# One fused attention and token-mixing kernel: the order of all work from a list scheduler in the program, evacuations on ACT or DVE by load, and kv from 65-column products

## The chip, the cores and the metric

The kernel runs on one core of one Trainium2 chip. The time is device microseconds of that core; the reported figure is a median of several executions. On one core a run more than 1.5% above the fastest of the same kernel counts as slow. The kernel before took 138.2 us (median of three runs, 137.22 to 140.5); the run that was profiled has a span of 134.9 us.

## The reference

Two stages. First a linear attention with cosine weights over 8 batches of 8 heads, 576 positions and 64 channels; then a token-mixing layer whose weights are computed from its own input.

```python
def phi(x, c, s):                        # c, s: cos and sin of pi/2 * position/576
    r = np.maximum(x, 0.0)
    return np.concatenate([r * c, r * s], axis=-1)
kv  = einsum('bhsf,bhsd->bhfd', phi(k), v);   z = sum over s of phi(k)
num = einsum('bhsf,bhfd->bhsd', phi(q), kv)
den = einsum('bhsf,bhf->bhs',  phi(q), z)[..., None] + 1e-06
x   = (num / den).transpose(0, 2, 1, 3).reshape(8, 576, 512)   # then, for each batch:
W   = 1/8 * (x @ w_q) @ (x @ w_k).T
out = relu(W @ x) @ w_out                # 8 x 576 x 512, float32
```

## The kernel before

Four heads are one step H (16 steps, two for a batch). A step goes: casts of q, k and v on GpSimd (POOL in the profile); kp = relu(k) times cosine and sine, on VectorE (DVE); a transpose of q on TensorE (PE) and its evacuation on DVE; the kv products on PE; the copy of kv to SBUF on ScalarE (ACT); two num products on PE; two norms on DVE. Two steps behind, the mixing layer of earlier batches runs in the gaps, and its output leaves as 36 row tiles of 128 rows (nine for a pair of batches, "1.5" is tile 5 of pair 1). The order of all this is written by hand as one loop. PE's results land in PSUM; copying them out to SBUF is called evacuation below. The tail is what follows the kv copy of the last step, H = 15. Loads and stores share one DMA queue, the one that SP issues, but for a k load at the start and five half stores at the end, which ACT issues.

```python
inp     = ctx.enter_context(tc.tile_pool(name="inp", bufs=4))      # raw q, k, v
prep    = ctx.enter_context(tc.tile_pool(name="prep", bufs=2))     # kp and rk
outpool = ctx.enter_context(tc.tile_pool(name="outpool", bufs=4))  # finished output tiles
...
def kv_mm(H, lo, hi):
    for c in range(lo, hi):
        for w in range(2):               # cosine or sine part
            for r in range(2):           # two halves of 64 rows, side by side in PE
                nc.tensor.matmul(        # 64 x (2 heads x 65) at once: 130 columns
                    bank(K0 + r)[:, 0, w * KW:(w + 1) * KW]...,
                    kp[H][half_rows(r), c, w, :],
                    v_bufs[H % 3][half_rows(r), c, :, 0:D + 1], ...)

def kv_evac(H, eng):
    kv_sb = small.tile([P, 2, 2 * KW], BF16, name="kv_sb")
    copy(eng, kv_sb, bank(K0, 2)[:, :, 0:2 * KW])       # one copy of 520 elements
...
def wout(bp, rt0, n, m, eng, qs=(nc.sync, nc.sync)):
    o_sb = outpool.tile([P, 2, DM], FP32, name="o_sb")
    ...                                  # four matmuls a row tile
    copy(eng, o_sb[:, 0:n, :], o_ps)
    ...                                  # two stores of 64 rows, from SP
```

Half of each kv product isn't used: it also multiplies one head's keys with the other head's values.

## Time and profile before

| | PE | DVE | ACT | POOL |
|---|---|---|---|---|
| busy, us of 134.9 | 109.3 | 91.4 | 74.3 | 71.1 |
| what fills it | matmuls of all stages | q evacuation, norm, kp | copies out of PSUM | casts of q, k, v |

First the groups of instructions (line, engine, operation, shapes, count | busy us, mean ns of one | idle before and who ended it), kv products and kp product:

```profile
L238 PE MATMUL ps<-v_buf,kp 64*128 64x130 bf16 x576 | 22.8, 218 | 8.4 <-DVE qpt_buf L230 5.6 <-issue 2.7
L201 DVE TENSOR_TENSOR kp<-rk,cossin 128x2304 bf16<-128x2304 bf16 x15 | 21.0, 1403 | 1.1 <-POOL rk L188 0.9
```

Then the list of waits (who <- for whom: us in total, times, longest), reduced to the one line in which an engine waits for a store:

```profile
ACT o_sb L175 <- DMA out_dram<-o_sb: 0.6, 1, 0.6
```

By the time a tile wants a buffer, its old store has landed, but once. And the clock row of the page, granted TensorE clock in tenths for 40 slices of 3.37 us:

```profile
PEclk9999968997799999999999999999999999999998
```

### The profile page before, as it was taken

The numbers are of one execution on the slowest core, as the hardware profiler recorded it, in microseconds if no ns is written. First come the engines' busy times: TensorE is split into PE (matmuls) and PEld (weight loads), VectorE is DVE, ScalarE is ACT, GpSimd is POOL, SyncE is SP. The second block draws the span as 40 slices with busy tenths as digits, with TensorE's granted clock in tenths as the row PEclk, the third lists the DMA queues.
The fourth block names the chain that finished last, engine by engine and source line by source line (L and its number), as shares of the span: only waits on it lengthen the run. The fifth ranks groups of instructions, "written<-read, shape, count | busy, mean of one in ns | idle before, by whom it ended". The sixth has DMA issues, their size and how long they took to land.

```text
span 134.9 us, 5317 instructions
## 1 busy us (share of the span) xinstructions
PE 109.3 (81%) x2276; PEld 69.5 (52%) x2276; DVE 91.4 (68%) x147; ACT 74.3 (55%) x126; POOL 71.1 (53%) x114
## 2 busy tenths in 40 slices
PE   5839399466669989999979794999998999898840
PEld 2216275344557656766665563666765675353410
DVE  1162979746798898879986968399879854334640
ACT  6941031307656766775766474658674776754310
POOL 7637865975999999637656565479521000000000
PEclk9999968997799999999999999999999999999998
DMA  3999999999999979999999999989955442287384
GB/s 102 361 385 392 372 355 390 386 390 389 388 384 393 392 225 301 367 385 395 374 357 376 322 357 388 372 249 353 238 202 118 109 94 66 57 256 177 81 248 137
DMA packets 21143, 39.40 MB, mean 292 GB/s; under 512 B 2944, under 2 KB 4480, under 8 KB 21120
## 3 DMA queue, kind: packets, MB, share of 16 engines
q1 hardware_dynamic: 20448, 38.08, 83.1%
q10 hardware_dynamic: 672, 0.98, 2.1%
q8 instruction: 18, 0.29, 1.0%
q14 instruction: 5, 0.04, 0.1%
HBM read 29.62 MB, written 9.44 MB: 290 GB/s over the span
## 4 chain that ended last, share of the span: by engine, by line
PE 40%; DMA 28%; ACT 9%; DVE 7%; issue 6%; POOL 5%; SPq 1%; ACTq 1%; DVEq 0%
PE ps L363 17%; DMA qf<-in_q_dram 10%; DMA vf<-in_v_dram 9%; DMA wo_f<-in_moe_w_out_dram 8%; PE ps L238 7%; PE ps L298 4%; PE ps L326 4%; ACT o_sb L175 4%; PE ps L257 3%; DVE qpt_buf L230 3%; ACT mix_sb L349 3%; POOL v_buf L213 2%; PE ps L341 2%; ACT wkj L175 1%; POOL rq_buf L188 1%
## 5 line engine op out<-in xcount | busy, mean ns | idle before, releaser
L363 PE MATMUL ps<-wo_sb,mix_sb 128*128 128x512 bf16 x144 | 36.0, 380 | 2.2 <-ACT o_sb L175 0.6
L213 POOL TENSOR_SCALAR v_buf<-vf 128x640 bf16<-128x640 f32 (+2 forms) x29 | 23.0, 811 | 16.3 <-DMA vf<-in_v_dram 9.2
L238 PE MATMUL ps<-v_buf,kp 64*128 64x130 bf16 x576 | 22.8, 218 | 8.4 <-DVE qpt_buf L230 5.6
L175 ACT COPY o_sb<-ps 128x512 f32<-128x512 f32 (+1 forms) x29 | 18.3, 630 | 19.6 <-PE ps L363 15.9
L188 POOL TENSOR_SCALAR rq_buf<-qf 128x640 bf16<-128x640 f32 (+2 forms) x31 | 23.7, 779 | 9.6 <-DMA qf<-in_q_dram 8.4
L201 DVE TENSOR_TENSOR kp<-rk,cossin 128x2304 bf16<-128x2304 bf16 (+2 forms) x17 | 22.6, 1327 | 7.1 <-ACT rk L186 6.0
L272 DVE TENSOR_TENSOR x_sb<-ps,rec 128x640 bf16<-128x640 f32 x32 | 26.4, 824 | 1.1
L238 PEld LDWEIGHTS <-kp 64*128 64x128 bf16 x576 | 18.8, 94 | 11.3 <-issue 6.9
L188 POOL TENSOR_SCALAR rk<-kf 128x640 bf16<-128x640 f32 (+2 forms) x29 | 20.8, 734 | 3.6 <-DMA kf<-in_k_dram 3.2
L230 DVE TENSOR_TENSOR qpt_buf<-ps,cst 128x1152 bf16<-128x1152 bf16 x32 | 22.6, 748 | 0.0
L363 PEld LDWEIGHTS <-mix_sb 128*128 128x128 bf16 x144 | 12.6, 97 | 15.2 <-issue 1.8
L349 ACT ACTIVATE mix_sb<-ps 128x576 bf16<-128x576 f32 x30 | 19.4, 654 | 1.4 <-PE ps L341 1.4
L175 ACT CAST kv_sb<-ps 128x520 bf16<-128x520 f32 x16 | 9.5, 592 | 17.8 <-PE ps L238 17.6
L257 PEld LDWEIGHTS <-qpt_buf 64*128 64x128 bf16 x640 | 13.3, 96 | 9.2 <-issue 8.7
L270 DVE RECIPROCAL rec<-ps 128x10 f32<-128x10 f32 x32 | 7.0, 219 | 16.1 <-PE ps L263 15.8
L257 PE MATMUL ps<-kv_sb,qpt_buf 64*128 64x65 bf16 x640 | 15.8, 194 | 1.9 <-ACT kv_sb L175 1.3
L175 ACT COPY xT_buf<-ps 128x512 bf16<-128x512 bf16 x16 | 9.4, 587 | 2.8 <-PE ps L284 2.7
L102 PE MATMUL ps<-warm 128*128 128x512 bf16 x28 | 9.3, 475 | 1.5 <-DVE warm L98 1.5
L298 PE MATMUL ps<-xT_buf,wqk_sb 128*128 128x288 bf16 x64 | 9.3, 286 | 1.2 <-ACT xT_buf L175 0.7
L341 PE MATMUL ps<-wT_buf,kx 64*128 64x288 bf16 x32 | 8.8, 289 | 1.2 <-DVE kx L177 0.5
L177 DVE COPY xT_buf<-ps 128x640 bf16<-128x640 bf16 x16 | 7.7, 483 | 2.3 <-PE ps L284 2.3
L341 PE MATMUL ps<-wq,kx 64*128 64x288 bf16 x32 | 8.8, 290 | 0.0
(50 smaller groups left out, 98.2 us busy)
## 6 DMA issues: line engine op xcount, KB each, us to landing
qf<-in_q_dram SPq DMA_DIRECT2D x15, 576.0 KB, 7.1
kf<-in_k_dram SPq DMA_DIRECT2D x15, 576.0 KB, 8.0
vf<-in_v_dram SPq DMA_DIRECT2D x15, 576.0 KB, 7.7
out_dram<-o_sb SPq DMA_DIRECT2D x55, 128.0 KB, 3.9
out_dram<-o_sb SPq DMA_DIRECT2D x6, 256.0 KB, 5.3
wo_f<-in_moe_w_out_dram SPq DMA_DIRECT2D x1, 1024.0 KB, 11.3
out_dram<-o_sb ACTq DMA_DIRECT2D x5, 128.0 KB, 2.7
kf<-in_k_dram ACTq DMA_DIRECT2D x1, 320.0 KB, 4.4
```

The costliest lines, as they stand in the source:

```text
L175: nc.scalar.copy(dst, src)
L188: eng.tensor_scalar(dst, src, FMAX, 0.0, op0=ALU.min, op1=ALU.max)
L201: nc.vector.tensor_mul(kp[H][:, lo:hi], rks[H][:, lo:hi].rearrange("p c i d -> p c (i d)").unsqueeze(2) .to_broadcast([P, hi - lo, 2, 2 * D]),
L213: eng.tensor_scalar(dst, src, 1.0, 1.0, op0=ALU.mult, op1=ALU.mult)
L230: nc.vector.tensor_mul(qpt_bufs[H % 2][:, r, :, D:SLOTS * D], bank_h(K0 + r)[:, 0:1, 0:HC].to_broadcast([P, 2, HC]), cst)
L238: nc.tensor.matmul(bank(K0 + r)[:, 0, w * KW:(w + 1) * KW].rearrange("p (i e) -> p i e", i=2), kp[H][half_rows(r), c, w, :], v_bufs[H % 3] ...
L257: nc.tensor.matmul(nb[t][:, u, :], qpt_bufs[H % 2][half_rows(t), r, w, u * P:(u + 1) * P], kvs[H][half_rows(t), r, o:o + D + 1], start=(u ...
L272: nc.vector.tensor_tensor(xv[:, h, r], nv[:, :, :, 0:D], rec.to_broadcast([P, 2, SC, D]), op=ALU.mult)
L298: nc.tensor.matmul(bank(m + nh)[:, 0, 0:hs], wqk_sb[:, dmc, :, :], xT_bufs[b % 2][:, dmc, nh * hs:(nh + 1) * hs], start=(dmc == 0), stop=( ...
L341: nc.tensor.matmul(bank(m + r)[:, 0, 0:hs], kxs[b][half_rows(r), i * P:(i + 1) * P], rhs, start=True, stop=True)
L349: nc.scalar.activation(dst, src, AF.Relu, scale=scale_moe)
L363: nc.tensor.matmul(o_ps[:, r, :], mixs[bp][:, dmc, rt * P:(rt + 1) * P], wo_sb[:, dmc, :], start=(dmc == 0), stop=(dmc == NDM - 1))
```

## The change

Its intent: a list scheduler in the program, fed with a cost for every piece of work and its dependencies, orders everything, so that each engine always takes the piece that can start soonest. Each copy out of PSUM may go to ACT or DVE, whichever the plan sees free. The kv products have 65 columns, the used half only; the sine part then lies in the other 64 partitions, and two small copies move it.

```diff
+PLAN = dict(mk=1.5, pa=3.218, pc=3.9, pm=3.2, pw=1.86, pb=0.0, flex=.163, poe=4.5, ...)
+def plan_order(NB, par=None):
...
+    op(("load", nm, H), {"DMA": 1.51}, [ago(H > 4, "r" + nm, H - 4)])
+    op(("mk", H), {"DVE": par["mk"]}, [("rk", H), ago(H > 1, "kv", H - 2)], par["pmk"])
+    op(("kve", H), {"ACT": 1.05, "DVE": .8}, [("kv", H)], 3)
...
+    op(("wo", p, rt), {"PE": .86}, need, pw, "full", 1)
+    op(("oe", p, rt), {"ACT": .60, "DVE": .71}, [("wo", p, rt)], par["poe"], ...)
+    op(("st", p, rt), {"DMA": .67}, [("oe", p, rt)])
...
     def kv_mm(H):
+        for c in range(C9):
+            for i in range(2):
                 for r in range(2):
                     nc.tensor.matmul(
+                        bank(K0 + r)[:, 0, i * (D + 1):(i + 1) * (D + 1)],
+                        kp[H][half_rows(r), 2 * c + i, :, :],
+                        v_bufs[H % 3][half_rows(r), c, i, 0:D + 1], ...)
     def kv_evac(H, eng):
+        copy(eng, kv_sb, src[:, :, 0:KW])                       # 260 elements
+        copy(eng, kv_sh[0:64], src[64:128, :, 0:D + 1])         # 130
+        copy(eng, kv_sh[64:128], src[0:64, :, D + 1:KW])        # 130
...
     def wout_evac(bp, rt, m, eng):
+        o_sbs[bp, rt] = outpool.tile([P, DM], FP32, name="o_sb")   # bufs=4, as before
...
+    for n, eng, m in plan_order(NB):
+        emit(n, eng, None if m is None else M0 + m)
```

"mk" (the kp product) waits for the kv products two steps back because there are two kp buffers. The output evacuation "oe" has no such line for its four buffers.

## The prediction

> **What bounds the kernel now.** I read the page's busy rows first, then its slices, then windows of the last third, then the order of time on single engines.
>
> ```profile
> PE 109.3 (81%) x2276; PEld 69.5 (52%) x2276; DVE 91.4 (68%) x147; ACT 74.3 (55%) x126; POOL 71.1 (53%) x114
> ...
> PE   5839399466669989999979794999998999898840
> ...
> DMA  3999999999999979999999999989955442287384
> GB/s 102 361 385 392 372 355 390 386 390 389 388 384 393 392 225 301 367 385 395 374 357 376 322 357 388 372 249 353 238 202 118 109 94 66 57 256 177 81 248 137
> ```
>
> A slice is 134.9 / 40 = 3.37 us. The DMA row is full from slice 2 to about slice 30 (100 us), then idles. PE has holes up to about 43 us and is then nearly full until 129 us. So two bounds follow each other: loads, then matrix work. DVE, at 68%, looks harmless on average. By stage it is not:
>
> ```profile
> 90.00:95.00 5.00, 4.89 (x131) 3.54 (x131) 4.44 (x8) 3.87 (x6) 3.93 (x5) 1.00 0.95 314
> ...
> 100.00:105.00 5.00, 4.42 (x106) 2.68 (x98) 4.92 (x8) 2.98 (x6) 1.31 (x2) 1.00 0.47 111
> ...
> 110.00:115.00 5.00, 4.77 (x74) 2.55 (x74) 1.88 (x4) 3.19 (x7) 0.00 (x0) 1.00 0.37 86
> ```
>
> (The last column is GB/s; the engines are PE, PEld, DVE, ACT, POOL.) In 100 to 105 us DVE is busy 4.92 of 5 us. After the last attention block (110 us) it has little to do. In order of time, ACT's copies of kv date the 16 attention steps H = 0 to 15:
>
> ```profile
> 51.23 0.59 ACT L175 CAST kv_sb<-ps 128x520 bf16<-128x520 f32 x1 [1.21 <-PE ps L238]
> 57.14 0.59 ACT L175 CAST kv_sb<-ps 128x520 bf16<-128x520 f32 x1
> ...
> 85.18 0.59 ACT L175 CAST kv_sb<-ps 128x520 bf16<-128x520 f32 x1
> ...
> 110.10 0.59 ACT L175 CAST kv_sb<-ps 128x520 bf16<-128x520 f32 x1
> ```
>
> These are H = 6, 7, 11 and 15: some 6.5 us a step. From 110.1 on PE works 18.7 us more (last matmul 128.8), then 6.1 us of copy, store and end. Whatever the change does early only counts if it moves the 110.1 or shortens these 25 us.
>
> **What the skill says.** (1) "TensorE: Matmul & The Clock Gate", section "Wait — 56ns, not 53.3ns?": warm matmuls start N / 2.4 GHz + about 2.5 ns apart, so 57 ns at 130 columns and 30 ns at 65. The trace agrees if the two 64-row halves run as a pair: 35 products of 130 columns took 1.20 us up to the end of the last (17.5 pairs of 57 ns are 1.0, and one is 0.22 long), and 20 num products of 65 columns pass in 0.31 us (31 ns a pair). (2) "ScalarE: Activation LUTs", section "What ACT_TABLE_LOAD costs": an ACTIVATE with immediate scale and bias takes 186 ns + 0.833 ns an element. Here 520 elements took 592 ns and 256 took 373: slope 0.83, constant 160; I use 160. (3) "VectorE: DVE Perf Modes", section "Mode 2×_1P — pack two bf16 into one 32-bit read": two results a cycle with 16-bit, unit-step operands. The kp product (2304 elements, 1403 ns, 0.61 ns each) agrees; runs of 64 in place of 128 should not change it.
>
> **The change, part by part.**
> Kv products: 576 stay 576, with 65 columns for 130. A step goes from about 1.2 to 0.6 us: 16 x 0.55 = 8.8 us of PE removed, all before 110 us, none in the tail.
> Kv copy: one of 520 elements becomes 260 + 130 + 130: 377 + 268 + 268 = 913 ns on ACT, +0.32 us on the kv-to-num chain and 14 x 0.32 = 4.5 us of ACT busy (two steps go to DVE). The chain gets 0.6 shorter on PE, so it breaks even or better.
> Kp product, q evacuation, norm: unchanged on DVE (1403, 2 x 748, 219 + 824 ns). Start to start they are a little shorter:
>
> ```profile
> 48.49 1.41 DVE L230 TENSOR_TENSOR qpt_buf<-ps,cst 128x1152 bf16<-128x1152 bf16 x2
> 49.82 0.21 DVE L270 RECIPROCAL rec<-ps 128x10 f32<-128x10 f32 x1
> 50.06 0.82 DVE L272 TENSOR_TENSOR x_sb<-ps,rec 128x640 bf16<-128x640 f32 x1
> 50.80 1.46 DVE L201 TENSOR_TENSOR kp<-rk,cossin 128x2304 bf16<-128x2304 bf16 x1
> ```
>
> A q pair is 1.33 us, a norm 0.98, a kp 1.35 (busy 1.40, its end overlapped by the next): 1.35 + 1.33 + 2 x 1.0 = 4.7 us of DVE a step.
> Order: loads run ahead. In the built order the first output store stands behind the load of q for H = 10 (before: of k for H = 8), and the last v load still has 25 of 36 row tiles' stores behind it.
> Output tiles: still four buffers. The scheduler's list gives an output evacuation one dependency only, its matmuls. The built program adds the real one: the fifth evacuation (now on DVE) waits until the first store has **landed**, the sixth (ACT) for the second, and so on. All stores are in the same queue as the loads.
>
> That is the step I weigh most. Landing times follow from bytes. The first 12 slices sum to 4294 x 3.37 = 14.5 MB by 40.5 us, at 388 GB/s in the last six. An offset of about 1.0 us from bytes to start comes from q of H = 1 (2.36 MB, reached at 8.8 us):
>
> ```profile
> 9.84 1.15 POOL L188 TENSOR_SCALAR rq_buf<-qf 128x1152 bf16<-128x1152 f32 x1 [2.16 <-DMA qf<-in_q_dram]
> ```
>
> Through the first row tile's store: ten steps of 3 x 0.59 MB, weights 1.31, q 0.59, store 0.26 = 19.9 MB, so 40.5 + 5.4 / 0.388 + 1 = 55.3 us. DVE would want that evacuation at about 47 us (my chaining of row durations: kv of H = 4 near 33 us for 38, since ACT's four wo casts no longer stand before kv of H = 3). So I expect DVE, and then PE behind it, to idle some 8 us, throwing away the early lead; kv of H = 7 comes near 60 (before 57).
> The same repeats: row tile 1.5 (DVE) waits for store 1.1, which has 15 steps, two loads, weights and 11 stores up to its end: 31.9 MB, 40.5 + 17.4 / 0.388 + 1 = 86.4 us. After it DVE, in order, has 9 norms (9.0), 5 q pairs (6.7), 3 kp (4.0), 2 wq copies (0.7), one kv copy (0.9), one xT (0.4), the evacuation itself (0.65): 22.4 us before kv of H = 15 can start, so 108.8, and 109.4 with its products. Before it was 110.1. Of the 8.8 us of PE removed, under 1 arrives.
> Tail: 14 output row tiles are left after kv of H = 15, before 13: 18.7 + 0.95 = 19.7 us. The nine last evacuations are all on ACT (0.59 each), which also issues five half stores (0.54 each), against 0.93 a tile on PE: about 1 us of lag. 109.4 + 19.7 + 6.1 + 1 = 136.2 us of span against 134.9; in the metric 138.2 x 136.2 / 134.9 = 139.5. I take 138.5, because DVE may be packed closer, or the stores land sooner, than I chained.
>
> **Rivals.**
> A: the store waits hardly bite, because DMA interleaves better than one queue in order. Then PE or DVE sets the pace: kv of H = 6 near 44 us and 9 steps of 5.4 give 93, plus 27 is 120 of span, 123 us. For it: POOL, ACT and PE have room. Against it: the waits are in the built program and the bytes cannot come earlier.
> B: worse than mine. ACT's own waits (tiles 1.2, 1.3, 1.6 before kv copies of H = 10 and 11) hold PE, whose clock row already shows less than full after early holes; 3 to 5 us more, 142 to 144. For it: ACT is in order and carries nearly all copies. Against: DVE needs that time anyway.
> C: the DVE-only limit without gaps from 55.3 on: 8 kp (10.8), 17 norms (17.0), 9 q pairs (12.0), 4 wq copies (1.3), 5 xT (2.1), 2 output copies (1.3), one kv (0.9), 45.4 us to kv of H = 15, so 101, + 26.8 = 128 of span, 131 us. It needs store 1.1 before 80 us, beyond 388 GB/s.
>
> **Range and chances.** My sum says 139.5, C's floor 131, B 144; the tuned-looking constants of the plan suggest that someone saw a gain, which I let pull a little. Range 131.5 to 143. Faster by over 2% (below 135.4) needs the waits to be smaller than the bytes say: 0.27. Slower by over 2% (above 141): 0.23. Within: 0.50.
>
> **What would show it.** Right: the fifth output evacuation on DVE and the sixth on ACT start only near 55 us with a DMA of an output store as releaser; a hole of several us in DVE and PE at 47 to 55; kv copies of H = 7 near 61, H = 10 near 85, H = 15 near 109; DMA row full without the dip of slice 15; kv products near 0.6 us a step; 900 ns for the three kv copies. Wrong: output evacuations that never wait for a DMA; kv of H = 15 before 103 us; or a tail much under 25 us.

## The result, and the profile after

The changed kernel takes 143.79 us (median of four runs, 142.93 to 144.09). The kernel before has 137.71 in the same comparison. The ratio of fast runs is 1.0462, with a 95% interval from 1.0385 to 1.0539: slower. (Such a ratio is the mean time of one kernel's fast runs over that of the other's fast runs of the same rounds, so it is not quite the ratio of the medians.) The range of the prediction ended at 143.0; the result lies just outside.

The page of the kernel after, busy row and the rows by slice (3.54 us each):

```profile
PE 111.5 (79%) x2257; PEld 66.1 (47%) x2279; DVE 97.9 (69%) x148; ACT 80.2 (57%) x159; POOL 64.2 (45%) x76
...
PE   5857688697999581897979479998899799989920
PEclk9999968965599959559999987999999999999995
DMA  4999999999999999999999999553333703857874
```

The same list of waits, for stores, after (14.4 us in all, where before it was 0.6):

```profile
ACT o_sb L329 <- DMA out_dram<-o_sb: 8.6, 4, 3.9
DVE o_sb L331 <- DMA out_dram<-o_sb: 5.8, 1, 5.8
```

The DMA row stays full through slice 25, without the dip that the kernel before had at slice 15: loads do run ahead. PE has two holes instead: slices 14 and 16, with the digits 5 and 1 (46 to 57 us), and slice 23 with the 4 (78 to 81 us). The views by time say whose they are. First hole, all engines in order of start (start us, duration, engine, line, operation, [idle before <- releaser]):

```profile
56.23 0.69 DVE L331 COPY o_sb<-ps 128x512 f32<-128x512 f32 x1 [5.78 <-DMA out_dram<-o_sb]
56.89 0.59 ACT L329 COPY o_sb<-ps 128x512 f32<-128x512 f32 x1 [3.89 <-DMA out_dram<-o_sb]
57.37 1.84 PE L456 MATMUL ps<-xT_buf,wqk_sb 128*128 128x288 bf16 x7 [3.60 <-DVE xT_buf L331]
```

Tile 0.4 on DVE is released by a store at 56.23, tile 0.5 on ACT right after, PE last: it had waited for a piece of DVE's that stands behind the tile. Second hole:

```profile
81.21 0.59 ACT L329 COPY o_sb<-ps 128x512 f32<-128x512 f32 x1 [3.42 <-DMA out_dram<-o_sb]
82.13 0.29 PE L502 MATMUL ps<-wT_buf,kx 64*128 64x288 bf16 x1 [2.74 <-ACT kx L329]
86.32 1.15 POOL L367 TENSOR_SCALAR v_buf<-vf 128x1152 bf16<-128x1152 f32 x1 [4.58 <-PE ps L391]
86.34 2.33 DVE L355 TENSOR_TENSOR kp<-rk,cossin 128x2304 bf16<-128x2304 bf16 x1 [1.39 <-PE ps L391]
89.06 0.69 DVE L331 COPY o_sb<-ps 128x512 f32<-128x512 f32 x1
```

ACT's tile 1.2 waits for a store, PE waits for the kx copy behind it, and DVE and POOL wait for PE's kv products. DVE's kp product then takes 2.33 us, because POOL's cast started 0.02 us before it, and tile 1.5 comes at 89.06. The attention steps, dated by ACT's kv copies of H = 6, 7, 11 and 15 as before:

```profile
50.21 0.38 ACT L329 CAST kv_sb<-ps 128x260 bf16<-128x260 f32 x1
64.57 0.38 ACT L329 CAST kv_sb<-ps 128x260 bf16<-128x260 f32 x1 [0.63 <-PE ps L391]
...
92.88 0.38 ACT L329 CAST kv_sb<-ps 128x260 bf16<-128x260 f32 x1 [0.21 <-PE ps L391]
...
115.40 0.38 ACT L329 CAST kv_sb<-ps 128x260 bf16<-128x260 f32 x1 [0.42 <-PE ps L391]
```

One step, from 50.21 to 64.57, takes 14.4 us. Before, H = 15 came at 110.10; now at 115.40, and 26.3 us follow (before 24.8). The windows that the prediction showed of before (PE, PEld, DVE, ACT, POOL, clock, DMA share, GB/s), here of after:

```profile
90.00:95.00 5.00, 4.87 (x144) 3.55 (x145) 4.90 (x7) 3.54 (x9) 3.53 (x4) 1.00 0.74 161
100.00:105.00 5.00, 4.46 (x126) 3.25 (x120) 4.82 (x8) 3.70 (x9) 0.00 (x0) 1.00 0.33 69
110.00:115.00 5.00, 4.00 (x148) 2.98 (x142) 4.10 (x9) 3.35 (x6) 0.00 (x0) 1.00 0.50 107
```

From 110 to 115 us DVE is still busy with attention, which it had left behind in the kernel before. The groups, kp product and kv products:

```profile
L355 DVE TENSOR_TENSOR kp<-rk,cossin 128x2304 bf16<-128x2304 bf16 x15 | 25.9, 1726 | 4.1 <-POOL rk L342 2.0 <-PE ps L391 1.8
L391 PE MATMUL ps<-v_buf,kp 64*128 64x65 bf16 x576 | 14.2, 199 | 3.1 <-DVE qpt_buf L383 3.1
```

PE's kv products fell from 22.8 to 14.2 us, as intended. The kp product, which nobody changed in size, rose from 1403 to 1726 ns. The Trainium skill's page "SBUF — State Buffer", section "Who interferes with whom", says why it can: a DVE instruction with two SBUF inputs contends with a GpSimd instruction that reads SBUF, and the ports that they share are an exclusive lock. The trace agrees, if DVE, second to start, waited for POOL to end: from POOL's end at 86.32 + 1.15 = 87.47 to DVE's end at 86.34 + 2.33 = 88.67 are 1.20 us, and a free kp product takes 1.35. The prediction had not used that page.

### The profile page after: what moved, and what is told of

It reads as the page before. It is cut to its first block, busy times and chain, and to the rows that moved or that the text cites. A ratio compares the mean times of both kernels' runs of the same rounds, so it can differ in the third digit from the quotient of the medians.

```text
span 141.7 us, 5312 instructions
## 1 busy us (share of the span) xinstructions
PE 111.5 (79%) x2257; PEld 66.1 (47%) x2279; DVE 97.9 (69%) x148; ACT 80.2 (57%) x159; POOL 64.2 (45%) x76
## 4 chain that ended last, share of the span: by engine, by line
DMA 51%; PE 19%; issue 9%; DVE 7%; ACT 4%; POOL 3%; ACTq 2%; SPq 1%; POOLq 0%; DVEq 0%
DMA qf<-in_q_dram 13%; DMA kf<-in_k_dram 12%; PE ps L526 10%; DMA wo_f<-in_moe_w_out_dram 9%; DMA wq_f<-in_moe_w_q_dram 8%; DMA vf<-in_v_dram 6%; DMA out_dram<-o_sb 3%; ACT o_sb L329 2%; PE ps L416 2%; DVE qpt_buf L383 2%; ACTq L536 2%; POOL rk L342 2%; PE ps L456 1%; PE ps L502 1%; PE ps L486 1%
## 5 line engine op out<-in xcount | busy, mean ns | idle before, releaser
L329 ACT COPY o_sb<-ps 128x512 f32<-128x512 f32 x34 | 20.0, 588 | 23.2 <-PE ps L526 13.4
L342 POOL TENSOR_SCALAR rq_buf<-qf 128x1152 bf16<-128x1152 f32 (+2 forms) x17 | 20.6, 1214 | 18.2 <-PE ps L377 10.2
L367 POOL TENSOR_SCALAR v_buf<-vf 128x1152 bf16<-128x1152 f32 x15 | 20.6, 1375 | 14.8 <-PE ps L391 11.7
L416 PEld LDWEIGHTS <-qpt_buf 64*128 64x128 bf16 x640 | 15.1, 99 | 15.0 <-issue 13.9
L342 POOL TENSOR_SCALAR rk<-kf 128x1152 bf16<-128x1152 f32 x15 | 19.0, 1270 | 1.5 <-DMA kf<-in_k_dram 1.4
L416 PE MATMUL ps<-kv_sh,qpt_buf 64*128 64x65 bf16 x320 | 17.1, 198 | 1.1
L329 ACT COPY xT_buf<-ps 128x512 bf16<-128x512 bf16 (+1 forms) x24 | 15.1, 643 | 2.8 <-PE ps L441 2.2
L391 PE MATMUL ps<-v_buf,kp 64*128 64x65 bf16 x576 | 14.2, 199 | 3.1 <-DVE qpt_buf L383 3.1
L391 PEld LDWEIGHTS <-kp 64*128 64x128 bf16 x576 | 11.8, 100 | 7.4 <-issue 3.3
L329 ACT CAST kv_sb<-ps 128x260 bf16<-128x260 f32 x14 | 5.3, 378 | 14.3 <-PE ps L391 14.1
L329 ACT CAST wT_buf<-ps 128x576 bf16<-128x576 f32 x8 | 5.1, 639 | 8.9 <-PE ps L456 8.9
```

The lines of the kernel that those rows point to most:

```text
L329: nc.scalar.copy(dst, src)
L342: eng.tensor_scalar(dst, src, FMAX, 0.0, op0=ALU.min, op1=ALU.max)
L367: eng.tensor_scalar(dst, src, 1.0, 1.0, op0=ALU.mult, op1=ALU.mult)
L391: nc.tensor.matmul(bank(K0 + r)[:, 0, i * (D + 1):(i + 1) * (D + 1)], kp[H][half_rows(r), 2 * c + i, :, :], v_bufs[H % 3][half_rows(r), c, ...
L416: nc.tensor.matmul(nb[t][:, u, :], qpt_bufs[H % 2][rows, r, w, u * P:(u + 1) * P], mv, start=(u == 0 and w == 0), stop=False)
```

## The experiments

Sixteen different kernels (two of them again in more rounds) test what the waits for stores, the kv part, the kp product, the choice of engine and the tail each do. All gave correct results.

### e1: twelve output buffers

```diff
-    outpool = ctx.enter_context(tc.tile_pool(name="outpool", bufs=4))
+    outpool = ctx.enter_context(tc.tile_pool(name="outpool", bufs=12))
```

> The changed kernel with 12 output buffers in place of 4, nothing else. Theory (the evacuations of the output projection wait for stores that stand behind loads): the 5.8 us wait of DVE at 56 us and ACT's 8.6 us of waits for output stores vanish, the kv copies of H = 7 and H = 15 come near 52 and 97 us (64 and 115 in the changed kernel), and the time falls to 124 to 130 us, below the kernel before. Rival 1 (the loss comes from slower DVE products of kp, 1613 ns for 1403, the PE clock and the three-part kv copy): the time stays at 140 or more. Rival 2 (loads running ahead is itself the harm, since stores are late whatever the buffers): 135 to 139, with a longer tail.

133.11 us (132.72 to 133.38, four runs), 10.7 us under the changed kernel, and under every run of the kernel before in all rounds (lowest 134.69). Tile 0.4 and tile 1.5 on DVE, and the kv copy of H = 15, in e1:

```profile
52.00 0.69 DVE L331 COPY o_sb<-ps 128x512 f32<-128x512 f32 x1 [1.36 <-PE ps L526]
...
79.01 0.67 DVE L331 COPY o_sb<-ps 128x512 f32<-128x512 f32 x1
...
105.22 0.38 ACT L329 CAST kv_sb<-ps 128x260 bf16<-128x260 f32 x1 [0.37 <-PE ps L391]
```

In its list of waits no engine waits half a microsecond for a store any more, and kv of H = 15 comes 10.2 us earlier. So the waits for stores carry the whole loss. But note 79.01 to 105.22: 26.2 us, in a kernel without any such wait; the prediction packed this stretch into 22.4 + 0.6.

### e2: stores taken before loads; e4: both

The other way to get stores out earlier: when a store and a load could start alike, the plan takes the store.

```diff
-                    key = s - par["pb"] * o["prio"]
+                    key = s - par["pb"] * o["prio"] - (.01 if n[0] == "st" else 0)
```

> The changed kernel with 4 output buffers, but the scheduler takes a store before a load where both could go. Theory: the first store is issued before the load of q for H = 7 or so and lands near 46 us, so the fifth evacuation hardly waits; 127 to 133 us; the DMA row may dip where the queue waits for an evacuation. Rival 1: 140 or more. Rival 2: it gains too, but no more than to 136, since the queue then stands still for stores.

> Both: 12 output buffers and stores before loads. Theory: no evacuation waits for a store in either, so the same as with 12 buffers alone within 2 us, 124 to 131. If loads running ahead matters in itself (rival 2), this one is clearly faster than 12 buffers alone; if the queue standing still for stores matters, clearly slower.

151.07 us for e2 (149.19 to 153.57) and 150.53 for e4 with twelve buffers as well (149.07 to 151.84). Both are far worse, and alike, so buffers are not what hurts here. The GB/s row of e2's page (its profile fell on a slow run, span 151.6; the fast runs are as bad):

```profile
GB/s 122 374 390 391 342 391 388 388 391 291 27 177 350 351 313 222 109 259 370 367 290 167 302 373 301 296 309 344 201 297 312 7 69 71 176 175 128 207 227 134
```

and from its list of waits, the first line for SP, which issues the queue, and two of the engines:

```profile
SPq L536 <- ACT o_sb L329: 48.2, 22, 12.9
...
DVE kp L355 <- POOL rk L342: 18.6, 8, 5.2
POOL v_buf L367 <- DMA vf<-in_v_dram: 17.1, 11, 3.1
```

SP issues in order, and a store that stands early waits for its evacuation, once 12.9 us long; every load behind it waits too (27 GB/s in slice 11). POOL then waits for v and DVE for POOL. e4's profile, of a fast run, has 47.1 us in this line. In the changed kernel the same line of SP's reads 22.3 us: there the stores stand late and the buffers pay, with stores early the loads pay. More buffers (e1) take the one away without the other.

### e3: the kv part alone, in the order before

The kernel before with cossin, the kp layout, the kv products, the three copies and num's operands as in the change.

> The kernel before with its own order and engines, and only the kv part of the change: 65-column products, three-part kv copy, sin parts moved. Theory (this part is good, about 0.5 us of PE a step, where PE is full): 132 to 136 us, ratio 0.96 to 0.985, kv products near 0.6 us a step, copies 0.92 us. Rival 1 (the kv part costs more than it saves, through the copy chain and ACT): 138 to 142. Rival 3: no change, 137 to 138, since DMA sets the pace up to 100 us.

138.59 us; the two fast runs are 137.69 and 136.78, the two fast runs of before in the same rounds 137.58 and 135.87. No gain is to be seen from 22.8 - 16.2 = 6.6 us less of kv products. Its granted clock was 0.56 at 30 to 40 us (before 0.83) and 0.76 at 40 to 50 (before 1.00), in a profile of a slow run, so I do not call that the cause.

### e5 and e6: more kp and v buffers, against the collision of DVE and POOL

```diff
-    prep = ctx.enter_context(tc.tile_pool(name="prep", bufs=2))
+    prep = ctx.enter_context(tc.tile_pool(name="prep", bufs=3))
-    for i in range(3):      # v_bufs, used as v_bufs[H % 3]
+    for i in range(5):      # v_bufs[H % 5]
```

e5 has this and twelve output buffers, e6 has this alone.

> As e1 (12 output buffers), and three buffers each for kp and rk (before 2), five for v (before 3), so that GpSimd's work on v and VectorE's kp product are no longer released by the same kv products. Theory (lock): kp product's mean falls from 1549 ns towards 1403, the v cast's from 1479 towards 1150, kv copy of H = 15 comes at 101 to 103 us in place of 105.2, time 129.5 to 131.5 (e1 133.1). Rival 1 (the two meet as often, only at other times): kp mean stays within 50 ns of 1549 and the time at 132.5 to 133.5. Rival 2 (the kp product gets short but VectorE then waits for PE, whose clock is what is short): kp mean falls, time stays within 0.7 us of 133.1.

> The changed kernel with its four output buffers, and only the three kp/rk and five v buffers. Theory (of the 6 us by which kv of H = 15 came later than predicted, some 3 are the longer kp products): kp mean falls from 1726 towards 1400 to 1500 ns, the fifth output evacuation still waits to 55 to 56 us for its store, kv copy of H = 15 near 112 to 113 (115.4), time 140 to 141.5 (143.8). Rival (after a wait for a store everything is late by that wait alone): time 143 to 144.5 whatever kp does.

133.74 us for e5 (fast runs 132.77 to 133.81) and 143.38 for e6 (fast runs 142.0 and 142.59). As a ratio to before, e6 is at 1.048, the changed kernel at 1.0462. The kp product did get shorter, in e6 from 1726 to

```profile
L355 DVE TENSOR_TENSOR kp<-rk,cossin 128x2304 bf16<-128x2304 bf16 x15 | 22.0, 1468 | 2.0 <-POOL rk L342 1.9
```

but the time did not follow as the theories had it. e6's two fast runs lie between its theory (140 to 141.5) and its rival (143 to 144.5), and its interval, 1.029 to 1.0669, leaves room for a gain of 1 to 2 us. e5 tests little: kp's mean fell only from 1549 in e1 to 1489, while POOL's cast of v rose from 1479 to 1719, so there the two still meet and POOL pays. (Both profiles are of slow runs, so only means of instructions are read from them; the times are those of the fast runs.)

### e7 and e16: the kv part undone in the new order

e7 is e1 with 130-column products and the single kv copy; e16 has the tail of e11 as well.

> As e1, but the kv products with 130 columns, one kv copy of 520 elements and cossin as before the change: what the kv part is worth in the new order. Theory (PE has slack, the kv-to-num chain is as long either way; the part is worth little, as e3 showed in the old order): time within 1 us of e1 (132.1 to 134.1). Rival (PE is short of time in the new order, at its low clock in the first 60 us above all): 8.8 us of PE return and 3 to 6 of them show: 136 to 139.

> 12 buffers and the tail of e11, with the kv products and the kv copy as before the change (e7), whose granted clock was 0.99 in all of e7's runs. If the kv part is worth about 1 us as e7 against e1 said: 132 to 134, 0.5 to 1.5 above e15. If the full clock makes up for it: within 0.5 of e15, with a narrower spread.

134.37 us for e7 (133.88 to 135.05), 1.3 us over e1, in different rounds; 134.19 for e16 (fast runs 133.06 to 134.94, one slow), 1.4 us over the two fast runs of e15 (below) in the same rounds. So in the new order the kv part is worth about 1.3 us of the 7.3 us of PE's kv products that it removes here (21.1 in e7, 13.8 in e1). What is striking is the clock. The page of e7:

```profile
PEclk9999999999999999999999999999999999999997
```

Its four runs have mean clocks of 0.974 to 0.995, e1's 0.936 to 0.969, e16's 0.976 to 0.993. With the 65-column products the clock tends to be lower, in e1 against e7 as in e3 against the kernel before; but the groups overlap (a fast run of e15, 65 columns, had 0.984). How much of the missing 6 us that explains no run here separates: e7 was slower even at nearly the full clock.

### e8: one fixed engine for each kind of evacuation

```diff
-        op(("kve", H), {"ACT": 1.05, "DVE": .8}, [("kv", H)], 3)
+        op(("kve", H), {"ACT": 1.05}, [("kv", H)], 3)
```

and so on for all kinds: ACT, but DVE for the second half of xT, as in the kernel before. The scheduler orders anew.

> As e1, but each kind of evacuation fixed to one engine, as in the kernel before (xT's second half on DVE, all others ACT), the scheduler's order made anew for that. Theory (choice by load matters only in the tail, where e1 has seven mix evacuations and one kx on DVE beside ACT's output tiles): kv of H = 15 within 1 us of e1's 105.2, tail 2 to 4 us longer, time 135 to 137. Rival (ACT had room for these too): 132.5 to 134.

137.76 us (137.0 to 138.4), 4.6 us over e1. The kv copy of H = 15 comes at 104.01, even before e1's 105.22; the tail is 30.9 us in place of 26.0. In it PE is the engine that is full (7.94 of 8 us from 120 to 128). From 104 us on the profile has 64 matmuls of output tiles in e8 and 52 in e1, that is 16 tiles and 13. So the choice by load pays in part through the order: with one engine for each kind, the plan leaves three more output tiles behind the last attention step. They are 2.7 us of PE (16.6 for 13.9) of the 4.9 us by which the tail is longer; the rest is not explained.

### e9 and e10: which of the two rounds of waits dates the end

In e9 the nine tiles of the first pair have a pool of their own, in e10 those of the second; all others share four buffers.

```diff
+    outown = ctx.enter_context(tc.tile_pool(name="outown", bufs=9))
-        o_sbs[bp, rt] = outpool.tile([P, DM], FP32, name="o_sb")
+        pool = outown if bp == 0 else outpool          # e10: bp == 1
+        o_sbs[bp, rt] = pool.tile([P, DM], FP32, name="o_sb")
```

> The changed kernel, with nine output buffers of their own for the first pair's tiles (0.0 to 0.8); all later tiles share four as before. The wait of tile 0.4 (56.2 us) is thus gone, the waits of tiles 1.4 and on for the stores of 1.0 and on stay. Theory (as the prediction had it, the second wait alone dates what follows: tile 1.5 may not start before store 1.1 lands at 86 to 87 us, by the bytes in the queue): no hole at 50 to 56 us, a longer one before 86 us, kv of H = 15 at 111 to 115, time 140 to 143 (143.8). Rival (the first hole is the loss; without it stores land early enough): 134 to 137.

> The changed kernel, with nine buffers of their own for the second pair's tiles (1.0 to 1.8); the first pair's share four, and tile 0.4 waits to 56 us. Theory (after the first hole the kernel runs as e1 does after its tile 0.4, which came at 52.0): kv of H = 15 at 109 to 110, 4 us after e1's, time 136.5 to 138.5. Rival 1 (the second wait was slack, since work catches up after it): 142 to 144. Rival 2 (the first hole is made up for later): 133 to 135.

e9: 144.52 us (143.0 to 144.94), as slow as the changed kernel although its first hole is gone. In order of time, tiles 1.4 and 1.5:

```profile
86.50 0.58 ACT L330 COPY o_sb<-ps 128x512 f32<-128x512 f32 x1 [8.75 <-DMA out_dram<-o_sb]
88.61 0.69 DVE L332 COPY o_sb<-ps 128x512 f32<-128x512 f32 x1 [10.92 <-DMA out_dram<-o_sb]
```

DVE had been ready at 77.7 us and stands 10.92 us. The lead of the first 50 us is simply lost here instead of there. e10: 139.84 us (138.82 to 140.52), so with the first hole only (tile 0.4 at 56.18) the kernel loses 6.7 us against e1, the second round adds 4 to that, and the second alone (e9) costs 11.4. (These are differences of medians, of different rounds.) The two costs don't add up: the queue sets a date for each, and work that is late for the first date is less early for the second.

### e13 and e14: DVE's waits alone, ACT's waits alone

In e13 tiles 0.0 and 0.4 share a buffer, 1.1 and 1.5 another, all other tiles have ten. In e14 tiles 0.4 and 1.5 have a buffer each, all others share four.

```diff
+        pool = (outw1 if (bp, rt) in ((0, 0), (0, 4)) else             # e13
+                outw2 if (bp, rt) in ((1, 1), (1, 5)) else outpool)
+        o_sbs[bp, rt] = pool.tile([P, DM], FP32, name="o_sb")
```

> The changed kernel, with buffers so that only the two evacuations on DVE wait for a store, as in the prediction's sum: tiles 0.0 and 0.4 share one buffer, 1.1 and 1.5 another, all other tiles have ten. ACT's waits for stores (tiles 0.5, 1.2, 1.3, 1.6) are gone. Theory (Rival B of the prediction was the missing part: ACT's waits came on top of DVE's): tile 0.4 still at 55 to 56.5 us, tile 1.5 at 86 to 87.5, kv of H = 15 at 110 to 112, time 138.5 to 140.5, 3 to 5 under the changed kernel's 143.8. Rival (ACT's waits are covered by DVE's, the miss comes from longer kp products and PE's clock): 142.5 to 144.5.

> The mirror of e13: the two tiles that DVE evacuates (0.4 and 1.5) have a buffer each of their own, all others share four, so that only ACT waits for stores, for 0.5 the first one. Theory (ACT, in order, holds PE and so DVE as well; either engine's waits reach the other within a step): 140 to 143.5. Rival (only DVE, the busier engine, matters): 134 to 137.

e13: 142.77 us (fast runs 142.15 to 143.1), ratio 1.0438. e14: 143.88 us (143.64 to 144.7). So my theory for e13 fell, its rival held: ACT's waits on top of DVE's are worth about 1 us by the medians, and by the ratios (1.0438 and 1.0462) nothing that their intervals can tell. (Before 95 us ACT no longer waits for stores in e13; 2.3 us of such waits, none over 1.0, are left after that.) Yet ACT's waits by themselves cost as much as DVE's: as the two holes above show, either engine, in order, holds the other through PE. e13 also has the date of the store that the prediction had worked out as 86.4, read where DVE stands and waits for just that store:

```profile
87.93 0.69 DVE L333 COPY o_sb<-ps 128x512 f32<-128x512 f32 x1 [3.13 <-DMA out_dram<-o_sb]
```

From there to its kv copy of H = 15 (115.05) are 27.1 us.

### e11, e12 and e15: the tail and the warm-ups

e11 is e1 with the last five output tiles alternating between DVE and ACT and the very last split in two, as in the kernel before; e15 is the same kernel in more rounds. e12 adds warm-up matmuls (46 in the profile in place of 31):

```diff
-            if gap > .9 and bank[3] <= free[e]:
-                order.append((("warm", int(gap / .45)), "PE", None))
+            if gap > .35 and bank[3] <= free[e]:
+                order.append((("warm", int(gap / .3)), "PE", None))
```

> As e1, but of the last five output tiles the even ones are fixed to DVE and the odd ones to ACT, the last one split between both, as in the kernel before. Theory (the last tiles wait for ACT, which evacuates all and issues half of the stores: PE idles 0.66 us before the last tile and the last evacuation starts 0.8 us after the last matmul): the tail gets 0.8 to 1.5 us shorter, time 131.6 to 132.5 (e1 133.1). Rival (the end is set by the last store's landing, whose queue is behind anyway): 132.8 to 133.4.

> The kernel of e11 again, in five rounds, since two of its four times were 3.5 us above the others. If the tail's repair is worth what the faster two say: median 131 to 132.5 and 3 to 4 per cent under the kernel before's fast runs. If the slower two are its usual time: 133 to 135, and the repair of the tail is worth nothing.

> As e11, with more warm-up matmuls: wherever the plan sees PE idle over 0.35 us with bank 7 free (before 0.9), one for each 0.3 us (before 0.45); some 40 in place of 18, all before kv of H = 3. Theory (the clock of 0.56 to 0.59 at 32 to 40 us follows PE's holes before it): clock over 0.8 there, kv copy of H = 5 at 40.5 to 41.5 us in place of 42.5, time 0.5 to 1.5 under e11. Rival (the early stage waits for loads and DVE, so a quicker PE changes nothing, or the clock falls elsewhere): within 0.5 us of e11.

e11 fell into two groups, 131.4 and 131.64 (fast) and 135.08 and 135.34 (slow); e15 again, 132.46 and 132.59, and four runs of 134.78 to 136.14. Its medians, 133.36 and 134.9, are no better than e1's. Whether the tail's repair is worth something stays open: in fast runs it may be 1.0 us (e15 against e17, below) to 1.6 (e11 against e1), but six of this kernel's ten runs were slow, and none of the ten of e1 and its repetition. e12 came out at 135.73 us (135.02 to 136.42). All four count as fast, since the rule goes by a kernel's own fastest run; but they lie where the slow runs of e11 and e15 lie (134.78 to 136.14), so e12 may have met the slow state throughout, and the time is no verdict on the warm-ups. The clock at 24 to 28 us (the third number from the end) in e11, in e15, which is the same kernel, and in e12:

```profile
24.00:28.00 4.00, 2.29 (x48) 1.64 (x49) 3.77 (x6) 1.24 (x3) 3.56 (x4) 1.00 1.05 390
...
24.00:28.00 4.00, 3.24 (x48) 2.05 (x48) 3.84 (x6) 0.91 (x2) 3.36 (x4) 0.57 1.05 390
...
24.00:28.00 4.00, 3.57 (x51) 2.09 (x50) 3.93 (x7) 0.75 (x2) 3.46 (x3) 0.62 1.05 390
```

It was 1.00 in one execution and 0.57 in another of one and the same program, so e12's 0.62 can't be put down to its warm-ups, nor PE's 3.57 us: at the lower clock some 50 matmuls keep PE busy longer than at the higher. The kv copy of H = 5 came at 43.85 in e12, at 43.47 in e15, at 41.49 in e11. So the theory (a clock over 0.8 at 32 to 40 us, a shorter time) did not come true: at 36 to 40 us the clock was 0.50 in e12 as in e15 (0.80 in e11). Whether more warm-ups help or harm stays open.

### e17 and e18: the best version again, and time taken off DVE

e17 is e1 in five rounds. e18 moves the eight copies of wq (0.3 us on DVE when free, 5.1 us in all in e1) to ACT, with the order made anew.

```diff
-        nc.vector.tensor_copy(wq2[64:128], wT_bufs[b % 2][0:64, D:SLOTS * D])
+        nc.scalar.copy(wq2[64:128], wT_bufs[b % 2][0:64, D:SLOTS * D])
```

> The kernel of e1 again, in five rounds, to stand beside e15 and e16: if e1's narrow spread holds, median 132.7 to 133.5, ratio of fast runs 0.97 to 0.98. If it falls into two groups as e15 did: a lower one near 132.5 to 133 and an upper one near 135 to 136.

> As e1, but the eight copies of wq go from VectorE (0.3 us when free, 1.1 us when GpSimd is at work, 5.1 us in all in e1) to ACT (some 0.65 each), the order made anew. Theory (between tile 1.5 and kv of H = 15 every step needs about 5.9 us because VectorE and PE wait for each other, so time taken off VectorE comes back as idle time, as with kp in e5 and e6): within 1 us of e17. Rival (VectorE is the bound, 1.5 to 3 us come off): 130 to 131.5.

e17: 133.63 us (132.62 to 134.41, six runs), ratio 0.9672 to the fast runs of before (95% interval 0.9593 to 0.9751). The record's own class for this comparison, as for all the experiments that have a ratio, is "unclear"; the interval lies wholly below 1. This is the version that beats both kernels. e18: one run of 130.76 and five slow, 133.4 to 135.1. It stays open whether DVE's time by itself is the limit.

## Why the prediction was right and wrong

The prediction said 138.5 us, most likely no change, and named waits for stores as the step that eats the gain. That mechanism is right, and e1 shows it: without these waits the kernel is 3% faster than before (e17). The time came out 5.3 us higher. By its own steps:

| step | predicted | changed kernel | what decides |
|---|---|---|---|
| tile 0.4 released by the first store | 55.3 | 56.23 | right (the hole on DVE before it: 5.8 us, not 8) |
| kv of H = 7 | near 60 | 64.57 | off, without effect on the end (e9) |
| tile 1.5 | 86.4 | 89.06 | 87.93 where only its own store holds it (e13) |
| tile 1.5 to the kv copy of H = 15 | 23.0 | 26.3 | the failed step |
| rest of the span | 26.8 | 26.3 | right |
| span | 136.2 | 141.7 | |

(23.0 is 109.4 - 86.4.) The 5.5 us of span are thus 2.7 of a late tile 1.5, 3.3 of a longer stretch, and 0.5 back in the tail. Other signs held: H = 10 at 86.27 (85 said), 378 + 2 x 263 = 904 ns for the three kv copies (900 said); the kv products took 0.74 us a step at full clock (near 0.6 said).

The path to tile 1.5 was not the one foretold. In the changed kernel DVE doesn't wait for store 1.1 at all: it comes to the tile at 89.06 straight from other work, late because ACT's wait for a store (tile 1.2) had held PE, PE held DVE (1.92 and 1.39 us), and kp then took 2.33. Only in e13, without ACT's waits, does DVE stand there for its own store, until 87.93. That both ways end within 1.1 us of each other is luck for the prediction.

**The kv part.** "Of the 8.8 us of PE removed, under 1 arrives" holds roughly: PE's kv products fell by 8.6 us, and e7 finds 1.3 us in the time, e3 none.

**The landing times.** Worked out from bytes in one ordered queue, 55.3 and 86.4; where DVE stood waiting, 56.09 to 56.23 and 87.93 to 88.61. The page "DMA: Bandwidth & Descriptors", section "Queues, rings and completion order", of the Trainium skill says that each engine of a queue consumes its descriptors in order and that the completion mark lands only after that engine's earlier writes. The trace agrees, with landings 0.8 to 2.2 us later than worked out. It is the safest part of the prediction, and the one that most decided it.

**The failed step** is "After it DVE, in order, has 9 norms (9.0), 5 q pairs (6.7), 3 kp (4.0), ... 22.4 us before kv of H = 15 can start". It lays DVE's instructions end to end. In the changed kernel the work from 89.06 to the end of the last q pair takes 25.4 us: the three kp products take 1.86, 2.33 and 1.36, together 1.5 more than the 4.05 that I gave them; DVE idles 0.30 and 0.70 for PE; the kv copy takes 1.10, not 0.9; the rest, some 0.3, is in the small gaps. The way from there to the copy takes 0.96 where I had 0.6. That is 25.4 + 0.96 = 26.3 in place of 23.0.

The kp products look like the cause, and this is where I was caught a second time: in e1 the three take 4.4 us in place of 5.6, and the stretch is as long. The stretch from tile 1.5 to the kv copy of H = 15, worked out from the order of time on DVE in five profiles of fast runs (DVE idle: up to the last q pair):

| kernel | stretch | kp, three | DVE idle | waits for stores in the kernel |
|---|---|---|---|---|
| changed | 26.3 | 5.6 | 1.0 | both rounds |
| e10 | 26.3 | 5.6 | 1.0 | first round |
| e1 | 26.2 | 4.4 | 1.2 | none |
| e13 | 27.1 | 5.9 | 1.3 | DVE's |
| e9 | 28.3 | 6.0 | 2.3 | second round |

It is never under 25.8 (e15, also without waits, with kp at 4.4) in a fast profile. But e1 doesn't clear the collision with POOL: there it meets another instruction. A wq copy that starts at 82.03, 0.14 us after a cast of POOL's, takes 1.17 us, where both wq copies take 0.30 in the changed kernel, so DVE is busy hardly less in e1 (24.0 us) than in the changed kernel (24.4). The one kept trace with next to no collision in the stretch is e6's, of a slow run but at the full clock there: the three kp take 4.2 us, the wq copies 0.30 each, DVE idles 1.5, and the stretch is 25.3. So the collision is about 1 us of the 3.3 in that trace, and over 2 stay. DVE and PE hand work to each other in every step (q transpose, q evacuation, kv products, kv copy, num, norm), and from 88 to 112 us of the changed kernel DVE is busy 22.4 of 24 us and PE 22.2. (PE's ends are modelled, so its share is not as firm as DVE's.) With both above 92%, laying DVE's work end to end left PE's out.

For these the traces hint at PE's side. e7 and e16, with 130-column products in the same order, take 29.6 and 29.4 us for this stretch, over 3 more than e1, with DVE no busier (24.2 and 23.5 us; e1 24.0) and PE some 2.1 us busier (25.4 and 25.5; e1 23.3). And of the five above, the two longer ones are those with less than the full clock there, e13 (0.94) and e9 (0.84). But e7 and e16 also change the kv copy, so no run isolates PE's part or the handing over itself: what makes up the rest of the 3.3 us is argued and not shown.

**Rival A** (the waits do not bite) expected 123 us; e1, where they don't, takes 133.1. Rival A packed a step into 5.4 us, and e1's take (105.22 - 58.48) / 8 = 5.8; its step H = 7 came at 58.48, where Rival A had H = 6 near 44 (e1: 50.40).

**Rival B** had the right size, 142 to 144, for a reason that turned out small. ACT's waits do hold PE, 2.74 us at 82.13, but without them e13 gets back about 1 us at most. "Against: DVE needs that time anyway" was right; the time was lost in DVE and PE together, not in ACT.

**The early pace.** After the first hole kv of H = 7 took 8.3 us from tile 0.4 in place of some 5: PE had stood 3.60 us, and its wqk matmuls took 1.84 us at a clock of 0.57 from 56 to 64 us (1.15 at full clock, at 89.65 us). This agrees with the page "TensorE: Matmul & The Clock Gate", section "What's actually happening", that activity releases a clock that is throttled by default. e9, which has no such hole, ends as late, so it did not set the end.

**The estimate.** The sum was 136.2 us of span. Scaling by 138.2 / 134.9 gave 139.5, but the profiled run of before took 136.67 us, so 1.8 of that scaling's 3.3 us were the profile's own distance and the rest a disturbed median. On the profiled run's footing the sum says 138.0, near the 138.5 that I took for another reason ("DVE may be packed closer, or the stores land sooner, than I chained"). Both went the other way: the stretch took 26.3 us, not 23.0, and store 1.1 released DVE at 87.93 (e13), not 86.4. The chance of 0.23 for slower was too low.

## What to carry to other kernels

When a scheduler reorders work, ask of every buffer whether its reuse is a dependency of the plan, the landing of stores in a shared queue included: here eight more buffers of 2 KB a partition are the difference between 4.6% slower and 3.3% faster (telling the plan of the four was not tried). Running loads far ahead makes stores in the same queue land late, and moving the stores forward stops the loads, so the buffers have to grow with the lead. And where two engines hand work to each other and both are nearly full (here 93% and 92%), packing one of them end to end came out 3.3 us short of 26.3; a measured stretch of such a stage is the safer start.

## What the Trainium skill lacked or had wrong

- "SBUF — State Buffer", section "Who interferes with whom", agrees with the traces: kp product 2.33 us in place of 1.35 when POOL's cast started 0.02 us before it. The page doesn't say that a shorter kp may bring little: its mean fell from 1726 to 1468 ns in e6, and the ratio to before was 1.048, interval 1.029 to 1.0669 (changed kernel 1.0462).
- "TensorE: Matmul & The Clock Gate", section "What's actually happening": activity releases the throttle. What counts as activity for products of 65 and of 130 columns no page says: the mean clock was 0.936 to 0.969 in e1's runs, 0.974 to 0.995 in e7's. Nor can one execution decide it: at 24 to 28 us the same kernel had 1.00 (e11) and 0.57 (e15).
- "ScalarE: Activation LUTs", section "What ACT_TABLE_LOAD costs": 186 ns + 0.833 ns an element for an ACTIVATE with immediate scale and bias. The changed kernel's kv copies, which the profile lists as CAST, of 260 and of 130 elements took 378 and 263 ns, which is 161 and 155 ns of constant at that slope; its ACTIVATE of 576 elements (mix_sb) took 652, which is 172.
- No page gives a way to date a store that stands behind loads in one queue. Bytes ahead of it over the rate of the last slices, plus 1.0 us, gave 55.3 and 86.4 us; 56.1 to 56.2 and 87.9 to 88.6 were measured.
- No page warns that a store early in a queue holds the loads behind it while its data is being made: 27 GB/s in slice 11 of e2, where the changed kernel moves 392, and 151 us in place of 143.8.
